# Half of an attention kernel's value matmuls moved into four column groups of TensorE

## The chip, the cores and the metric

The kernel runs on one core of a Trainium2 chip. The time is the device time of one execution in microseconds (us), the median of several runs. TensorE multiplies matrices into PSUM, ScalarE (ACT) applies functions, VectorE (DVE) does element work, GpSimd (POOL) does slower element work, SyncE (SP) starts transfers.

## The reference

Two rounds of a transformer block over x of 2048 rows and 512 columns: attention with 32 heads of 16 columns, then a feed-forward network (FFN) of 1792, each behind a layer norm and added to x. Both rounds use the same weights.

```python
def _A_ref(x, wqkv, wo):
    qkv = (x @ wqkv).reshape(B, S, 3, H, Dh).transpose(2, 0, 3, 1, 4)
    scores = einsum("bhqd,bhkd->bhqk", q, k) * Dh ** -0.5
    o = einsum("bhqk,bhkd->bhqd", softmax(scores), v)
    return o.transpose(0, 2, 1, 3).reshape(B, S, D) @ wo
...
x = x + _A_ref(_layernorm(x), A_wqkv, A_wo)
x = x + _B_ref(_layernorm(x), B_w1, B_w2)   # silu(x @ w1) @ w2
x = x + _A_ref(_layernorm(x), A_wqkv, A_wo)
x = x + _B_ref(_layernorm(x), B_w1, B_w2)
```

## The kernel before

Each layer runs in four **stages**, one for each chunk c of 512 query rows. A stage has eight **head blocks** (hb, four heads at a time), and each of these has sixteen **units** (kt), one for each tile of 128 keys. So a layer has 4 x 8 x 16 = 512 units, in the order of the list `units` (loop at line 576).

A unit does this. Four score matmuls (line 520) take K and Q of four heads, which lie 32 partitions apart, 17 rows each (16 columns of the head and one row that carries an offset, so that the exponentials stay in range), and write scores of 128 keys by 512 queries for each head, two heads to a PSUM tile `s_ps`. Two exponentials on ACT (line 585) read these tiles, 1024 elements in a partition, and write `p_sb`. Four value matmuls (line 532) multiply them with the values into `o_ps`, 128 partitions by 512, which is summed over all sixteen key tiles. Head j of the four owns partitions 32j to 32j+16 there: 16 value columns and the softmax's denominator, from a column of ones.

For that, the values stand in **padded blocks** `vd`: for each key tile and head 128 columns that are zero except for the head's 17. Each value matmul thus writes all 128 partitions and adds zeros to three heads. POOL copies the values from `v` (columns of 16) into the blocks (`vd_fill`, line 138), four key tiles at a time (`NG = 4`) in a ring of two (`NR = 2`); the zeros and ones are set once.

The order of instructions on TensorE, ACT and VectorE is the program's own order. In a unit's iteration of the loop, ACT gets the unit's two exponentials; TensorE gets the scores of the **next** unit, then the value matmuls of the second half of the last unit and of the first half of this one (`pend`), then **filler** work. There are three PSUM buffers of scores (`spool`), so the scores run at most a unit and a half ahead, and five buffers for `p_sb`.

The filler is a queue of small steps (`Pump`): K of the next head block (two matmuls a step, line 225, in the first stage of a layer only), Q of the next head block (lines 298 to 327), and from the second stage on the output projection of the last chunk (lines 362 to 383), its layer norm (lines 149 to 195), its FFN (lines 392 to 405, with a tanh on ACT, line 429) and in layer 0 the next layer's norm and values (line 269). `todo` spreads the steps over the stage's units. The K and Q steps stand in front, so that in the first stage of a layer the last units of a head block have no filler.

At a head's **boundary** (kt = 0) the value matmuls of the last head block are finished; VectorE casts `o_ps` to `oT` (line 573); and the next step in the queue, four transposes on TensorE (line 336), waits for this cast. At kt = 0 no value matmul of the new head is issued; all four follow at kt = 1, with two of that unit.

Outside the stages, a layer begins with K, Q and V for the first units and ends with the last chunk's projection and FFN.

Of the kernel before, what the change touches and what calls it, by code (L numbers as in the profile page):

```python
# [18 lines left out]
def kernel(  # L19
# [10 lines left out]
    nc = tc.nc  # L30
# [15 lines left out]
    EPS = 1e-5  # L46
    VS = DH + 1
    NG = 4
    NR = 2

    cpool = ctx.enter_context(tc.tile_pool(name="cpool", bufs=1))
    wpool = ctx.enter_context(tc.tile_pool(name="wpool", bufs=1))
    xpool = ctx.enter_context(tc.tile_pool(name="xpool", bufs=1))
    xnpool = ctx.enter_context(tc.tile_pool(name="xnpool", bufs=2))
    xtpool = ctx.enter_context(tc.tile_pool(name="xtpool", bufs=4))
    vpool = ctx.enter_context(tc.tile_pool(name="vpool", bufs=2))
# [6 lines left out]
    tpool = ctx.enter_context(tc.tile_pool(name="tpool", bufs=1))  # L63
    small = ctx.enter_context(tc.tile_pool(name="small", bufs=4))
    spool = ctx.enter_context(tc.tile_pool(name="spool", bufs=3, space=bass.MemoryType.PSUM))
    oppool = ctx.enter_context(tc.tile_pool(name="oppool", bufs=1, space=bass.MemoryType.PSUM))
# [2 lines left out]
    def wide(name):  # L69
        return spool.tile([P, 2, 512], FP32, name=name, tag="s")  # L70

    def narrow(name):
        return gpool.tile([P, 512], FP32, name=name, tag="g")
# [16 lines left out]
        nc.gpsimd.memset(E[32 * j : 32 * j + 16, 32 * j + 16 : 32 * j + 17], -1.0)  # L90
    eps_t = cpool.tile([P, 1], FP32, name="eps_t")
    nc.vector.memset(eps_t[:], EPS)
    onescol = cpool.tile([P, 1], FP32, name="onescol")
    mc_ps = narrow("mc_ps")
    nc.tensor.matmul(mc_ps[:, 0:1], lhsT=cw[0:1, 0:128], rhs=cw[0:1, 128:129], start=True, stop=True)
    nc.vector.tensor_copy(out=onescol[:], in_=mc_ps[:, 0:1])


    x_sb = xpool.tile([P, TT, D], BF16, name="x_sb")
# [12 lines left out]
    for ct in range(CT):  # L112
        nc.gpsimd.tensor_copy(
            out=wk_pad[:, ct, :, 0:DH],
# [3 lines left out]
            out=wq_pad[:, ct, :, 0:DH],  # L118
# [9 lines left out]
    vs = [vpool.tile([P, TT, D], BF16, name=f"v{i}", tag="v") for i in range(2)]  # L128
    vdq = []
    for i in range(NR):  # L130
        vd = xpool.tile([P, NG, 4, P], BF16, name=f"vd{i}")
        nc.gpsimd.memset(vd[:], 0.0)
        for j in range(4):
            nc.gpsimd.memset(vd[:, :, j, 32 * j + DH : 32 * j + DH + 1], 1.0)
        vdq.append(vd)


    def vd_fill(va, hb, g, slot):
        for j in range(4):
            h = 4 * hb + j  # L140
            nc.gpsimd.tensor_copy(  # L141
                out=vdq[slot][:, :, j, 32 * j : 32 * j + DH],
                in_=va[:, NG * g : NG * (g + 1), DH * h : DH * (h + 1)],
            )


# [119 lines left out]
    def v_mm(xnT, tt, ps, cts):  # L266
        tq = tt % 4
        for ct in cts:
# [2 lines left out]
                start=(ct == 0), stop=(ct == CT - 1),  # L271
            )

    def v_piece(cellx, tt, va):
        cell = {}

        def a():
            cell["ps"] = narrow("v_ps")
            v_mm(cellx["xnT"], tt, cell["ps"][:, :], (0, 1))

        def b():
            v_mm(cellx["xnT"], tt, cell["ps"][:, :], (2, 3))
            nc.vector.tensor_copy(out=va[:, tt, :], in_=cell["ps"][:, :])

        return [a, b]

    def v_two(xnT, tt, va):
        ps = wide("v2_ps")
        for i in range(2):
            v_mm(xnT, tt + i, ps[:, i, :], range(CT))  # L290
        nc.vector.tensor_copy(out=va[:, tt : tt + 2, :], in_=ps[:, :, :])

    def q_piece(xnTs, c, hb, QTs):
        cell = {}

# [221 lines left out]
    def emit_s(QT, hb, kt):  # L517
        tiles = [wide("s_ps") for _ in range(2)]
        for j in range(4):
            nc.tensor.matmul(  # L520
                tiles[j // 2][:, j % 2, :],
                lhsT=KT[32 * j : 32 * j + VS, hb, kt * P : (kt + 1) * P],
                rhs=QT[32 * j : 32 * j + VS, :],
                start=True,
                stop=True,
            )
        return tiles

    def emit_pv(o_ps, p_sb, kt, pr):
        for jj in range(2):  # L530
            j = 2 * pr + jj
            nc.tensor.matmul(  # L532
                o_ps[:, :],
                lhsT=vdq[kt // NG % NR][:, kt % NG, j, :],
                rhs=p_sb[:, jj, :],
                start=(kt == 0 and j == 0),
                stop=(kt == TT - 1 and j == 3),
            )
# [11 lines left out]
    for L in range(2):  # L550
# [14 lines left out]
        attn = None  # L565
        o_ps = None
        pend = []
        s_now = emit_s(QTs[0][0], 0, 0)
        left = 0

        def finish_heads(o_ps, hb, attn):
            oT = opool.tile([P, 512], BF16, name="oT", tag="oT")
            nc.vector.tensor_copy(out=oT[:], in_=o_ps[:])  # L573
            pump.front([heads_piece(oT, hb, attn)], state["begun"])

        for u, (c, hb, kt) in enumerate(units):
            if kt == 0:
                if hb == 0:
                    old_attn, attn_c = (attn, c - 1)
                    new_attn = apool.tile([P, 4, D], BF16, name="attn", tag="attn")  # L580

            ps = []
            for pr in range(2):
                p_sb = ppool.tile([P, 2, 512], BF16, name="p_sb", tag="p")
                nc.scalar.activation(  # L585
                    p_sb[:].rearrange("p a b -> p (a b)"),
                    s_now[pr][:].rearrange("p a b -> p (a b)"),
                    ACT.Exp,
                    scale=float(SCALE),
                )  # L590
                ps.append(p_sb)

            if u + 1 < len(units):
                nc_, nhb, nkt = units[u + 1]
                s_now = emit_s(QTs[nc_][nhb], nhb, nkt)

            if kt == 0:
                for args in pend:
                    emit_pv(*args)
                pend = []  # L600
# [10 lines left out]
                pend = [(o_ps, ps[0], 0, 0), (o_ps, ps[1], 0, 1)]  # L611
# [9 lines left out]
                pump.q[at:at] = [list(p) for p in must]  # L621
                left = at + len(must)
            else:
                pend.append((o_ps, ps[0], kt, 0))
                for args in pend:
                    emit_pv(*args)
                pend = [(o_ps, ps[1], kt, 1)]

            if kt % NG == 0 and u > 0 and u + NG * (NR - 1) < len(units):
                _, fhb, fkt = units[u + NG * (NR - 1)]  # L630
                vd_fill(va, fhb, fkt // NG, fkt // NG % NR)

            remaining = TT * HB - (hb * TT + kt)
            total = pump.steps()
# [1 line left out]
            todo = -(-(total + later) // remaining) if total else 0  # L636
            if left and kt < TT - 2 and pump.q:
                todo = max(todo, 1)
            pump_some(todo)
# [5 lines left out]
        for args in pend:  # L645
            emit_pv(*args)
        finish_heads(o_ps, HB - 1, attn)
        run(pump.q)
        pump.q = []
# [34 lines left out]
```

## Time and profile before

| | |
|---|---|
| runs | 2186.79 us median of 3 (2185.69 to 2189.19) |
| profiled execution, span | 2190.4 us |
| TensorE matmul busy | 1952.9 us (89%), 10355 records |
| ACT busy | 1943.4 us (89%) |
| VectorE busy | 558.6 us (26%) |
| POOL busy | 248.2 us (11%) |
| exponentials (line 585) | 2048, 1920.4 us busy |
| value matmuls (line 532) | 3909 records, 1045.1 us busy, mean 386 ns |
| score matmuls (line 520) | 4096, 575.3 us busy, mean 385 ns |
| mean granted clock of TensorE | 0.968 |
| DMA | 5 GB/s over the span |

The span runs from the first to the last instruction of one profiled execution. Busy time merges overlapping instructions: the 4096 score matmuls of 385 ns add up to far more than 575 us, because four of them run side by side. An instruction's duration is its latency, so a row of matmuls that follow each other closely takes less time than the sum of the means. 4096 value matmuls are issued; some records are missing from the trace. The granted clock is the share of its full rate at which TensorE was let run. The chain of waits follows the end of the span back to what released each step.

### The profile page before, as it was taken

What the parts mean: (1) busy time and instruction counts of PE and PEld (TensorE: products, weight loads), DVE (VectorE), ACT (ScalarE), POOL (GpSimd) and SP (SyncE); (2) the same over time, 40 slices, a digit from 0 to 9 for tenths busy, and PEclk for the clock granted to TensorE, in tenths of its full rate; (3) what the DMA queues carried; (4) which work ended last, traced back from release to release, by engine and by line L of the source; (5) the groups of instructions that cost most, each with busy time, mean ns of one, the idle gap of its engine ahead of it and who ended that gap; (6) DMA issues with size and microseconds to landing.
All of it is one profiled execution on the core that took longest, in us unless ns stands there. A gap on an engine that the chain in (4) does not pass through costs nothing.

```text
span 2190.4 us, 28490 instructions
## 1 busy us (share of the span) xinstructions
PE 1952.9 (89%) x10355; PEld 717.0 (33%) x10561; DVE 558.6 (26%) x1106; ACT 1943.4 (89%) x2152; POOL 248.2 (11%) x1055
## 2 busy tenths in 40 slices
PE   3999988999889998899778999998999989998996
PEld 1333323333333333333222333333333333333332
DVE  6323212112311133112343323131113111131114
ACT  0899989999799997999517999999999999999981
POOL 3111101111011110111000111111111111111100
PEclk9999999999899998999878999999999999999997
DMA  4000000000000000000000000000000000000000
GB/s 144 1 1 1 1 1 1 1 1 1 1 1 1 1 1 1 1 1 1 1 0 1 1 1 1 1 1 1 3 8 1 1 1 8 4 1 1 6 5 10
DMA packets 8477, 11.79 MB, mean 5 GB/s; under 512 B 400, under 2 KB 7312, under 8 KB 8336
## 3 DMA queue, kind: packets, MB, share of 16 engines
q1 hardware_dynamic: 7280, 8.39, 1.1%
q8 instruction: 82, 1.34, 0.3%
q10 hardware_dynamic: 1056, 1.57, 0.2%
q14 instruction: 59, 0.48, 0.1%
HBM read 7.86 MB, written 2.10 MB: 5 GB/s over the span
## 4 chain that ended last, share of the span: by engine, by line
PE 64%; ACT 21%; issue 8%; DVE 6%; DMA 0%; ACTq 0%; DVEq 0%
PE o_ps L532 30%; ACT p_sb L585 19%; PE s_ps L520 17%; PE y_ps L399 3%; PE k_ps L225 3%; PE q_ps L298 3%; PE h_ps L392 2%; PE y_ps L371 2%; PE v_ps L269 2%; ACT t_sb L429 1%; DVE st L149 1%; PE t_ps L194 1%; DVE oT L573 1%; PE at_ps L336 1%; DVE hT L477 1%
## 5 line engine op out<-in xcount | busy, mean ns | idle before, releaser
L585 ACT ACTIVATE p_sb<-s_ps 128x1024 bf16<-128x1024 f32 x2048 | 1920.4, 1237 | 123.3 <-PE s_ps L520 123.3
L532 PE MATMUL o_ps<-p_sb,vd 128*128 128x512 bf16 x3909 | 1045.1, 386 | 19.7 <-issue 15.5
L520 PE MATMUL s_ps<-QT,KT 17*128 17x512 bf16 x4096 | 575.3, 385 | 89.6 <-ACT p_sb L585 85.3
L532 PEld LDWEIGHTS <-vd 128*128 128x128 bf16 x4096 | 318.8, 98 | 484.8 <-issue 246.8
L141 POOL COPY vd<-v 128x64 bf16<-128x64 bf16 x1024 | 231.5, 239 | 1868.1 <-PE o_ps L532 1723.6
L520 PEld LDWEIGHTS <-KT 17*128 17x128 bf16 x4096 | 175.1, 91 | 591.1 <-issue 571.2
L573 DVE CAST oT<-o_ps 128x512 bf16<-128x512 f32 x64 | 44.3, 692 | 380.3 <-PE o_ps L532 380.3
L430 DVE SCALAR_TENSOR_TENSOR hT<-t_sb,h_ps 128x512 bf16<-128x512 f32 x84 | 57.5, 684 | 301.5 <-ACT t_sb L429 301.5
L399 PE MATMUL y_ps<-w_sb,hT 128*128 128x512 bf16 x445 | 128.0, 388 | 5.4 <-DVE hT L477 4.5
L392 PE MATMUL h_ps<-xnT,w_sb 128*128 128x512 bf16 x438 | 126.6, 387 | 3.2 <-DVE hT L477 1.4
L313 DVE CAST qc<-q_ps 128x512 bf16<-128x512 f32 x64 | 44.2, 691 | 173.0 <-PE q_ps L298 173.0
L242 DVE TENSOR_SCALAR KT<-k_ps,onescol 128x512 bf16<-128x512 f32 x56 | 42.0, 750 | 172.1 <-PE k_ps L225 172.1
L194 PE MATMUL t_ps<-ident,xn 128*128 128x128 bf16 x256 | 32.2, 271 | 57.1 <-DVE xn L182 55.4
L405 DVE SCALAR_TENSOR_TENSOR x_sb<-y_ps,x_sb 128x512 bf16<-128x512 f32 x32 | 22.1, 690 | 232.7 <-PE y_ps L399 232.7
L476 ACT ACTIVATE t_sb<-h_ps 128x1024 f32<-128x1024 f32 x14 | 14.3, 1024 | 75.1 <-PE h_ps L392 59.0
L298 PE MATMUL q_ps<-xnT,wq_pad 128*128 128x512 bf16 x255 | 77.0, 385 | 2.5 <-DVE attn L343 2.4
L225 PE MATMUL k_ps<-xnT,wk_pad 128*128 128x512 bf16 x254 | 78.7, 402 | 0.3 <-issue 0.2
L429 ACT ACTIVATE t_sb<-h_ps 128x512 f32<-128x512 f32 x84 | 76.9, 916 | 0.0
L399 PEld LDWEIGHTS <-hT 128*128 128x128 bf16 x448 | 44.3, 100 | 61.4 <-issue 6.1
L392 PEld LDWEIGHTS <-w_sb 128*128 128x128 bf16 x448 | 44.7, 100 | 58.4 <-issue 8.3
L327 DVE CAST QT<-q_ps 128x512 bf16<-128x512 f32 x64 | 44.2, 691 | 37.0 <-PE q_ps L322 37.0
L371 PE MATMUL y_ps<-wo_sb,aT 128*128 128x512 bf16 x126 | 40.8, 425 | 7.5 <-DVE aT L366 7.3
(58 smaller groups left out, 572.8 us busy)
## 6 DMA issues: line engine op xcount, KB each, us to landing
w_sb<-in_B_w_dram SPq DMA_DIRECT2D x2, 1792.0 KB, 15.0
x_sb<-in_A_x_dram SPq DMA_DIRECT2D x4, 512.0 KB, 9.8
out_dram<-x_sb SPq DMA_DIRECT2D x16, 128.0 KB, 1.7
wraw<-in_A_wqkv_dram ACTq DMA_DIRECT2D x1, 1024.0 KB, 7.6
wv_sb<-in_A_wqkv_dram ACTq DMA_DIRECT2D x1, 512.0 KB, 10.0
wo_sb<-in_A_wo_dram SPq DMA_DIRECT2D x1, 512.0 KB, 12.3
```

The costliest lines, as they stand in the source:

```text
L141: nc.gpsimd.tensor_copy(out=vdq[slot][:, :, j, 32 * j : 32 * j + DH], in_=va[:, NG * g : NG * (g + 1), DH * h : DH * (h + 1)],)
L225: nc.tensor.matmul(ps, lhsT=wk_pad[:, ct, 4 * hb : 4 * hb + 4, :].rearrange("p h s -> p (h s)"), rhs=xnT[:, ct, :], start=(ct == 0), stop= ...
L298: nc.tensor.matmul(cell["ps"][:, :], lhsT=wq_pad[:, ct, 4 * hb : 4 * hb + 4, :].rearrange("p h s -> p (h s)"), rhs=xnTs[c][:, ct, :], star ...
L371: nc.tensor.matmul(cell["ps"][:, :], lhsT=cell["aT"][:, ct, :], rhs=wo_sb[:, ct, :], start=(ct == 0), stop=(ct == CT - 1),)
L392: nc.tensor.matmul(ps, lhsT=w1_sb[:, ct, ft * P : (ft + 1) * P], rhs=xfT[:, ct, :], start=(ct == 0), stop=(ct == CT - 1),)
L399: nc.tensor.matmul(ps, lhsT=hT[:, ft, tq * P : (tq + 1) * P], rhs=w2_sb[:, ft, :], start=(ft == 0), stop=(ft == FT - 1),)
L429: nc.scalar.activation(t_sb[:, 0, :], hc["ps"][:, :], ACT.Tanh, scale=0.5)
L430: nc.vector.scalar_tensor_tensor(out=cell["hT"][:, ft, :], in0=t_sb[:, 0, :], scalar=1.0, in1=hc["ps"][:, :], op0=ALU.add, op1=ALU.mult,)
L520: nc.tensor.matmul(tiles[j // 2][:, j % 2, :], lhsT=KT[32 * j : 32 * j + VS, hb, kt * P : (kt + 1) * P], rhs=QT[32 * j : 32 * j + VS, :], ...
L532: nc.tensor.matmul(o_ps[:, :], lhsT=vdq[kt // NG % NR][:, kt % NG, j, :], rhs=p_sb[:, jj, :], start=(kt == 0 and j == 0), stop=(kt == TT - ...
L573: nc.vector.tensor_copy(out=oT[:], in_=o_ps[:])
L585: nc.scalar.activation(p_sb[:].rearrange("p a b -> p (a b)"), s_now[pr][:].rearrange("p a b -> p (a b)"), ACT.Exp, scale=float(SCALE),)
```

## The change

The key tiles 1, 3, 5, ... 15 of each head block (`COL`) no longer use padded blocks. Their values are read from `va`, the values in columns of 17 (16 and a one, set once by POOL), 32 columns at a time, and each of the four matmuls writes only its own 32 partitions of `o_ps`. (The 15 columns behind a head's 17 belong to the next head; what they add to `o_ps` lies in partitions that nobody reads.) The even tiles (`DIAG`) keep the padded blocks, which now hold two tiles (`NG = 2`). Both halves of an odd unit's value matmuls go into the iteration after it, before the first half of the even unit's. Score matmuls read 32 rows for 17; the added rows are zero. V goes into `va` with one cast for each tile of 128 rows, two where one was. Q's last step adds a constant column, and the exponential takes the same amount off again by a bias column. A path for exponentials on VectorE (`OFF`, `exp_passes`) is written but its list is empty: it issues nothing, and `late` and `passes` stay empty.

```diff
-    NG = 4
+    NG = 2
     NR = 2
+    COL = [1, 3, 5, 7, 9, 11, 13, 15]
+    DIAG = [kt for kt in range(TT) if kt not in COL]
+    KR = 32
+    OFF = []
...
+    nshift = cpool.tile([P, 1], FP32, name="nshift")
+    nc.vector.memset(nshift[:], -SHIFT)
+    nc.vector.tensor_scalar_mul(out=ccol[:], in0=onescol[:], scalar1=SHIFT / SCALE)
...
+    VW = VS * H + 32 - VS
+    for i in range(2):
+        va = xpool.tile([P, TT, VW], BF16, name=f"va{i}")
+        nc.gpsimd.memset(va[:], 1.0)
...
     def vd_fill(va, hb, g, slot):
+        k0, step = DIAG[NG * g], DIAG[1] - DIAG[0]
-                out=vdq[slot][:, :, j, 32 * j : 32 * j + DH],
-                in_=va[:, NG * g : NG * (g + 1), DH * h : DH * (h + 1)],
+                out=vdq[slot][:, :, j, 32 * j : 32 * j + VS],
+                in_=va[:, k0 : k0 + step * (NG - 1) + 1 : step, VS * h : VS * h + VS],
...
-        nc.vector.tensor_copy(out=va[:, tt : tt + 2, :], in_=ps[:, :, :])
+        for i in range(2):
+            nc.vector.tensor_copy(
+                out=v_dst(va, tt + i), in_=ps[:, i, :].rearrange("p (h d) -> p h d", d=DH)
+            )
...
-            nc.vector.tensor_copy(out=QTs[c][hb][:], in_=cell["ps"][:, :])
+            nc.vector.tensor_scalar(
+                out=QTs[c][hb][:], in0=cell["ps"][:, :], scalar1=ccol[:, 0:1], scalar2=None,
+                op0=ALU.add,
+            )
...
-                lhsT=KT[32 * j : 32 * j + VS, hb, kt * P : (kt + 1) * P],
-                rhs=QT[32 * j : 32 * j + VS, :],
+                lhsT=KT[32 * j : 32 * j + KR, hb, kt * P : (kt + 1) * P],
+                rhs=QT[32 * j : 32 * j + KR, :],
...
+    def emit_pv(o_ps, ps, hb, kt, prs, va):
+                if kt in COL:
+                    h = 4 * hb + j
+                    nc.tensor.matmul(
+                        o_ps[32 * j : 32 * j + 32, :],
+                        lhsT=va[:, kt, VS * h : VS * h + 32],
+                        rhs=ps[pr][:, jj, :],
+                        start=False,
+                        stop=(kt == TT - 1),
+                        skip_group_check=True,
+                    )
...
+                        bias=nshift[:],
                         scale=float(SCALE),
...
             else:
-                pend.append((o_ps, ps[0], kt, 0))
-                for args in pend:
-                    emit_pv(*args)
-                pend = [(o_ps, ps[1], kt, 1)]
+                flush(u)
+                elif kt in COL:
+                    pend.append((o_ps, ps, hb, kt, (0, 1)))
+                else:
+                    emit_pv(o_ps, ps, hb, kt, (0,), va)
+                    pend.append((o_ps, ps, hb, kt, (1,)))
```

More of the change, by code (lines that the diff above doesn't have):

```diff
@@ L55 @@
     xtpool = ctx.enter_context(tc.tile_pool(name="xtpool", bufs=4))
-    vpool = ctx.enter_context(tc.tile_pool(name="vpool", bufs=2))
     qpool = ctx.enter_context(tc.tile_pool(name="qpool", bufs=3))
@@ L63 @@
     tpool = ctx.enter_context(tc.tile_pool(name="tpool", bufs=1))
+    epool = ctx.enter_context(tc.tile_pool(name="epool", bufs=1))
     small = ctx.enter_context(tc.tile_pool(name="small", bufs=4))
@@ L92 @@
     nc.vector.memset(eps_t[:], EPS)
+    LOG2E = 1.4426950408889634
+    POLY = (-0.15703108, 12.31057503, 23.05391661, 37.67973007)
+    SHIFT = (127.0 - 6.207248627973487) / LOG2E
+    nshift = cpool.tile([P, 1], FP32, name="nshift")
+    nc.vector.memset(nshift[:], -SHIFT)
     onescol = cpool.tile([P, 1], FP32, name="onescol")
+    ccol = cpool.tile([P, 1], FP32, name="ccol")
     mc_ps = narrow("mc_ps")
@@ L127 @@
     amax = xpool.tile([P, HB], FP32, name="amax")
-    vs = [vpool.tile([P, TT, D], BF16, name=f"v{i}", tag="v") for i in range(2)]
+    VW = VS * H + 32 - VS
+    vs = []
+    for i in range(2):
+        va = xpool.tile([P, TT, VW], BF16, name=f"va{i}")
+        nc.gpsimd.memset(va[:], 1.0)
+        vs.append(va)
     vdq = []
@@ L132 @@
         nc.gpsimd.memset(vd[:], 0.0)
-        for j in range(4):
-            nc.gpsimd.memset(vd[:, :, j, 32 * j + DH : 32 * j + DH + 1], 1.0)
         vdq.append(vd)
     def vd_fill(va, hb, g, slot):
+        k0, step = DIAG[NG * g], DIAG[1] - DIAG[0]
         for j in range(4):
@@ L272, in v_mm, with v_dst @@
             )
+    def v_dst(va, tt):
+        return va[:, tt, 0 : VS * H].rearrange("p (h s) -> p h s", s=VS)[:, :, 0:DH]
     def v_piece(cellx, tt, va):
@@ L282, in b @@
             v_mm(cellx["xnT"], tt, cell["ps"][:, :], (2, 3))
-            nc.vector.tensor_copy(out=va[:, tt, :], in_=cell["ps"][:, :])
+            nc.vector.tensor_copy(
+                out=v_dst(va, tt), in_=cell["ps"][:, :].rearrange("p (h d) -> p h d", d=DH)
+            )
         return [a, b]
@@ L290, in v_two @@
             v_mm(xnT, tt + i, ps[:, i, :], range(CT))
-        nc.vector.tensor_copy(out=va[:, tt : tt + 2, :], in_=ps[:, :, :])
+        for i in range(2):
+            nc.vector.tensor_copy(
+                out=v_dst(va, tt + i), in_=ps[:, i, :].rearrange("p (h d) -> p h d", d=DH)
+            )
     def q_piece(xnTs, c, hb, QTs):
@@ L515, in pump_some, with emit_s @@
             state["begun"] = pump.step()
-    def emit_s(QT, hb, kt):
-        tiles = [wide("s_ps") for _ in range(2)]
-        for j in range(4):
+    def emit_s(QT, hb, kt, pr):
+        s_ps = wide("s_ps")
+        for jj in range(2):
+            j = 2 * pr + jj
             nc.tensor.matmul(
-                tiles[j // 2][:, j % 2, :],
-                lhsT=KT[32 * j : 32 * j + VS, hb, kt * P : (kt + 1) * P],
-                rhs=QT[32 * j : 32 * j + VS, :],
+                s_ps[:, jj, :],
+                lhsT=KT[32 * j : 32 * j + KR, hb, kt * P : (kt + 1) * P],
+                rhs=QT[32 * j : 32 * j + KR, :],
                 start=True,
@@ L526, in emit_s @@
             )
[L527 to L537, printed above, removed]
-            )
+        return s_ps
+    def emit_pv(o_ps, ps, hb, kt, prs, va):
+        for pr in prs:
+            for jj in range(2):
+                j = 2 * pr + jj
+                if kt in COL:
[7 more added lines that the diff above has]
+                        skip_group_check=True,
+                    )
+                else:
+                    d = DIAG.index(kt)
+                    nc.tensor.matmul(
+                        o_ps[:, :],
+                        lhsT=vdq[d // NG % NR][:, d % NG, j, :],
+                        rhs=ps[pr][:, jj, :],
+                        start=(kt == 0 and j == 0),
+                        stop=False,
+                        skip_group_check=True,
+                    )
@@ new lines, in exp_passes, with horner, split, broken @@
+    def exp_passes(s_ps, p_sb):
+        z = epool.tile([P, 1024], I32, name="z", tag="z")
+        m = epool.tile([P, 1024], FP32, name="m", tag="m")
+        y = epool.tile([P, 1024], FP32, name="y", tag="y")
+        flat = "p a b -> p (a b)"
+        def horner(out, in0, k, in1):
+            nc.vector.scalar_tensor_tensor(
+                out=out, in0=in0, scalar=POLY[k], in1=in1, op0=ALU.add, op1=ALU.mult
+            )
+        def split():
+            nc.vector.tensor_scalar(
+                out=z[:], in0=s_ps[:].rearrange(flat), scalar1=float(SCALE * LOG2E * 2**23),
+                scalar2=0.0, op0=ALU.mult, op1=ALU.max,
+            )
+        def broken():
+            nc.vector.tensor_scalar(
+                out=m[:].bitcast(I32), in0=z[:], scalar1=0x7FFFFF, scalar2=0x3F800000,
+                op0=ALU.bitwise_and, op1=ALU.bitwise_or,
+            )
+        def whole():
+            nc.vector.tensor_scalar(
+                out=z[:], in0=z[:], scalar1=0x7F800000, scalar2=None, op0=ALU.bitwise_and
+            )
+        return [
+            split, broken, whole,
+            lambda: horner(y[:], m[:], 0, m[:]),
+            lambda: horner(y[:], y[:], 1, m[:]),
+            lambda: horner(y[:], y[:], 2, m[:]),
+            lambda: horner(p_sb[:].rearrange(flat), y[:], 3, z[:].bitcast(FP32)),
+        ]
@@ L567 @@
         pend = []
-        s_now = emit_s(QTs[0][0], 0, 0)
+        late = []
+        passes = []
+        s_now = [emit_s(QTs[0][0], 0, 0, pr) for pr in range(2)]
         left = 0
@@ L574, in finish_heads, with flush @@
             pump.front([heads_piece(oT, hb, attn)], state["begun"])
+        def flush(u):
+            for args in pend:
+                emit_pv(*args, va)
+            pend.clear()
+            while late and late[0][0] <= u:
+                emit_pv(*late.pop(0)[1], va)
         for u, (c, hb, kt) in enumerate(units):
@@ L578 @@
                 if hb == 0:
-                    old_attn, attn_c = (attn, c - 1)
                     new_attn = apool.tile([P, 4, D], BF16, name="attn", tag="attn")
+            off = kt in OFF
             ps = []
             for pr in range(2):
[L584 to L590, printed above, removed]
+                if pr == 1 and off:
+                    p_sb = epool.tile([P, 2, 512], BF16, name="pd_sb", tag="pd")
+                    new = exp_passes(s_now[1], p_sb)
+                    new.pop(0)()
+                    passes += new
+                else:
+                    p_sb = ppool.tile([P, 2, 512], BF16, name="p_sb", tag="p")
+                    nc.scalar.activation(
+                        p_sb[:].rearrange("p a b -> p (a b)"),
+                        s_now[pr][:].rearrange("p a b -> p (a b)"),
+                        ACT.Exp,
+                        bias=nshift[:],
+                        scale=float(SCALE),
+                    )
                 ps.append(p_sb)
+            nxt_s = []
             if u + 1 < len(units):
                 nc_, nhb, nkt = units[u + 1]
-                s_now = emit_s(QTs[nc_][nhb], nhb, nkt)
+                nxt_s = [lambda pr=pr: emit_s(QTs[nc_][nhb], nhb, nkt, pr) for pr in range(2)]
+            s_now = [f() for f in (nxt_s[:1] if off else nxt_s)]
             if kt == 0:
-                for args in pend:
-                    emit_pv(*args)
-                pend = []
+                flush(u)
+                assert not late
                 if o_ps is not None:
@@ L610 @@
                 o_ps = oppool.tile([P, 512], FP32, name="o_ps", tag="o")
-                pend = [(o_ps, ps[0], 0, 0), (o_ps, ps[1], 0, 1)]
+                pend.append((o_ps, ps, hb, kt, (0, 1)))
                 must = []
@@ L623 @@
             else:
-                pend.append((o_ps, ps[0], kt, 0))
-                for args in pend:
-                    emit_pv(*args)
-                pend = [(o_ps, ps[1], kt, 1)]
-            if kt % NG == 0 and u > 0 and u + NG * (NR - 1) < len(units):
-                _, fhb, fkt = units[u + NG * (NR - 1)]
-                vd_fill(va, fhb, fkt // NG, fkt // NG % NR)
+                flush(u)
+                if off:
+                    s_now += [f() for f in nxt_s[1:]]
+                    emit_pv(o_ps, ps, hb, kt, (0,), va)
+                    late.append((u + 7, (o_ps, ps, hb, kt, (1,))))
+                elif kt in COL:
+                    pend.append((o_ps, ps, hb, kt, (0, 1)))
+                else:
+                    emit_pv(o_ps, ps, hb, kt, (0,), va)
+                    pend.append((o_ps, ps, hb, kt, (1,)))
+            if passes and not off:
+                passes.pop(0)()
+            elif passes and len(passes) > 6:
+                passes.pop(0)()
+            nd = len(DIAG)
+            if kt in DIAG and DIAG.index(kt) % NG == 0 and u > 0:
+                at_d = (c * HB + hb) * nd + DIAG.index(kt) + NG * (NR - 1)
+                if at_d < NQC * HB * nd:
+                    fhb, fd = at_d // nd % HB, at_d % nd
+                    vd_fill(va, fhb, fd // NG, fd // NG % NR)
             remaining = TT * HB - (hb * TT + kt)
@@ L638 @@
                 todo = max(todo, 1)
+            if off:
+                todo = 0
             pump_some(todo)
@@ L644 @@
                     pump_some(1)
-        for args in pend:
-            emit_pv(*args)
+        flush(len(units) + TT)
         finish_heads(o_ps, HB - 1, attn)
```

## The prediction

> **What bounds the kernel now.** I read the rows of ScalarE's exponential line first, cut at the eight stages (four query chunks of 512 rows in each of two layers). Columns: window, its length, ACT busy (instructions), granted TensorE clock, DMA share, GB/s.
>
> ```profile
> 65.28:303.19 237.91, 235.16 (x257) 0.99 0.00 1
> 303.19:559.20 256.01, 241.99 (x258) 0.97 0.00 1
> ...
> 1161.34:1401.43 240.09, 235.20 (x257) 0.98 0.00 1
> 1401.43:1644.91 243.48, 240.93 (x258) 0.99 0.01 3
> ```
>
> ACT is busy almost throughout, and busy time alone does not say whether it is the limit. So I took the chain of waits in a stretch without filler work, where each unit shows one exponential and the next one starts when it should:
>
> ```profile
> 1220.16 1.29 ACT p_sb L585
> ...
> 1221.97 1.31 ACT p_sb L585
> ```
>
> Two exponentials take 1.81 us, 0.905 each. Where a tanh of the FFN stands between two, it adds 0.47 (ACT's timeline: tanh starts at 692.30, the exponential behind it at 692.77). The floor of a stage is therefore 256 x 0.905 = 231.7 us, with 14 tanhs 238.3. Excess over it: 6.2 in the first stage, 17.7 in each of the next three (53.3 in all), 8.4, 5.2, 3.9 and 4.3 in layer 1: **81 us**. Whatever TensorE is spared, no more can be won, and the 216 us outside the stages (65.3 of start, 89.9 between layers, 60.8 of end) hold no attention loop.
>
> Where the 81 us lie: the first 43.8 us of the stages at 303, 559 and 815 hold 32 exponentials (29.0), 14.8 lost each, 44.4 in all; the other 61 head blocks lose 36.9, 0.60 each. Inside a block TensorE with filler work runs at ACT's own pace, as the chain in layer 1 shows:
>
> ```profile
> 1206.78 0.43 PE s_ps L520 x4
> 1207.21 0.97 PE o_ps L532 x4
> 1208.18 0.43 PE k_ps L225 x2
> ```
>
> That is 1.83 us against 1.81. The 0.60 is lost at the head's boundary, where TensorE, in order, waits for VectorE's cast and then has six value matmuls before the next scores:
>
> ```profile
> 1225.55 0.55 PE o_ps L532 x2
> ...
> 1226.12 0.70 DVE oT L573
> ...
> 1226.87 0.40 PE at_ps L336 x4
> 1227.27 0.33 PE s_ps L520 x4
> 1227.60 1.40 PE o_ps L532 x6
> 1229.00 0.43 PE k_ps L225 x2
> ```
>
> **The clock** is the second thing to read. Columns: window, length, PE, PEld, DVE, ACT, POOL busy (instructions), granted clock.
>
> ```profile
> 1192.90:1196.30 3.40, 2.46 (x18) 0.69 (x17) 0.95 (x2) 3.40 (x5) 0.91 (x4) 1.00 0.00 0
> 1196.30:1199.70 3.40, 3.40 (x12) 0.98 (x8) 0.42 (x1) 2.11 (x3) 0.00 (x0) 0.50 0.03 5
> ...
> 1223.70:1227.11 3.41, 2.47 (x15) 0.78 (x14) 0.69 (x1) 3.41 (x5) 0.91 (x4) 1.00 0.00 0
> 1227.11:1230.53 3.42, 3.42 (x23) 1.31 (x21) 0.68 (x2) 3.26 (x4) 0.00 (x0) 1.00 0.00 0
> ```
>
> Two head boundaries, alike to a few hundredths; after one the clock is 0.50 for a window of 3.4 us, after the other it is not. The second holds some eight passes of 512 columns (six padded value matmuls, four scores side by side, the start of the transposes), 8 x 0.216 = 1.73 us, half of the window. So boundaries now sit at the edge of a threshold near one half.
>
> **The change part by part.** A padded value matmul takes 0.216 in a row (0.43 for two, filler rows). Two units, an odd and an even key tile, now take 3.66. After it:
> - The iteration of an odd tile: scores 0.43, two padded matmuls of the tile before 0.43, filler 0.43 = 1.29.
> - The iteration of an even tile: scores 0.43, the block of four narrow matmuls C, two padded 0.43, filler 0.43, and one more change of array mode. The scores' four matmuls are one pass of 0.22 (a lone pass: "q_ps L322 0.22") and take 0.43, so entering and leaving cost 0.21; one change is half, 0.10.
> - C is not in the trace: at least a pass, 0.22; at most four in a row, 0.97. I take 0.43, the scores' block, the nearest row, since it too is four narrow matmuls side by side. Then the even iteration is 1.82 and the pair 3.11, 0.55 less, far under ACT's 3.62.
>
> Inside a block this earns nearly nothing: ACT is late next, at 0.905. At a boundary the two matmuls become C (-0.12) and the six become four (-0.43); I count 0.43 of the 0.60. At full clock: 61 x 0.43 = **-26**. In the long openings (303, 559, 815) 16 units are eight pairs; five at full clock save 0.44 (the odd 0.97 becomes 0.53), two at half clock 0.86, one lies under the LN chain on VectorE (329.75 to 336.5): 3.9 each, **-12**.
>
> Against this stands the clock. In the boundary window above, six padded matmuls become two plus C: eight passes become five, 32% of the window. I found none this thin inside the stages that kept the clock. In the filler-free tail of a head of stage 0 a pair of units is seven passes in 3.62 us, 42%, also below the edge. What a half-clock window costs is measured: head blocks that have one last 31.2 us, the others 29.6: 1.6. Of the six padded matmuls that stood in it (2.66 against 1.40) four remain, which saves 0.85. A boundary at half clock then loses 0.60 + 1.6 - 0.85 = 1.35, 0.75 **more** than now; at full clock 0.43 less. Boundaries break even when 36% fall. I take all 14 of stage 0 (no filler in the tail) and a third of the 47 others, 30 of 61: 30 x 0.75 - 31 x 0.43 = **+9**. Four boundaries are cold today and save 0.85: **-3**.
>
> [...]
>
> Small parts. Weight loads: 98 ns each, under matmuls now; if those of the block lay open, 4 x 0.098 = 0.39 makes the pair 3.50, still below 3.62: 0. [...] Scores over 32 rows: matmuls of 17 and of 128 rows last 385 and 386 ns: 0. V's first cast, two of 512 for one of 1024: 2 x 0.691 - 1.225 = 0.157, x8: **+1**, at most, as TensorE sets that stretch. QT's add: 0.750 (the KT row) for 0.691, on an engine busy 26%: 0. The exponential's bias is another column of the same size; the page's fill of a 128x1 constant 0.0 is the one of before: 0. POOL: two fills of 8944 elements, by 3.52 per 4096, 7.7 each; POOL ends at 17.5 today and then at about 32, V's first cast is at 49: hidden by 17. POOL's copies stay 1024, now 34 elements for 64: 0. DMAs stay. A new wait: both tiles of an odd unit are read one iteration later, and the second exponential two units on needs the buffer (five in the ring). It starts 0.905 after the first, C ends 0.43 after the scores: free at full clock, about even at half. Behind it on ACT stand all exponentials, and TensorE's scores for them.
>
> Sum: -12 + 9 - 3 + 1 = -5. The profiled execution spans 2190.4, the median of the runs is 2186.8, 3.6 below: 2190.4 - 5 - 3.6 = **2182 us**. This kernel's measurement tells 0.2% (4.4 us) from no change.
>
> **The rivals.**
> - The clock holds (the narrow block counts as much as a padded one). For it: boundaries such as that at 1223.7 hold now. Against: five passes for eight. -26 - 12 - 8 (the four cold ones save 2.0 each) + 1 = -45: 2142.
> - Slower, one mechanism: TensorE, lighter, falls to half clock at every boundary and stays there for two windows in half of them, since waiting for VectorE's cast leaves the first half-clock window unfilled as well (the stage openings show pairs of such windows: 0.84 of clock over 43.8 us). In the second window a unit with filler takes about 2.6 us (1.56 doubled, less the waits that don't grow) for 1.81, 1.3 units: +1.0. 61 x 0.75 + 30 x 1.0 = 76, less 14: 2190.4 + 62 - 3.6 = 2249. It decides from about 15 us more than the 36% give, that is when 60% of the boundaries fall.
> - The narrow matmuls run one after another (C = 0.97): the change doesn't do what it says. The pair is 1.29 + 2.36 + 0.10 = 3.75, above ACT's 3.62, in 104 pairs with filler of the two stages 0 and 84 of the FFN's second product: 188 x 0.13 = +24, clock as now: 2212. For: no row shows column groups. Against: row groups do overlap (575 us for 4096 matmuls of 385 ns).
>
> **How the numbers follow.** Forecast (2168 to 2197) 0.42: faster 0.20, same 0.13, slower 0.09. Clock holds 0.22, faster. Two windows 0.20, slower. In a row 0.12, slower. The ring or the bias costs after all 0.04, slower. Together: faster 0.42, same 0.13, slower 0.45. The range 2145 to 2235 leaves out half of the first rival and half of the second.
>
> **What would show it.** The narrow block in the chain near 0.43 (0.22 to 0.97); exponentials at 1.81 per unit in all blocks; the span's mean clock below 0.968, with 0.50 windows behind most boundaries of stage 0 and a third of the others; head blocks of 29.2 where it holds and 30.3 where it falls; openings of about 40 instead of 43.8. It is wrong if the exponential's own pace moves, or if the clock falls in the middle of blocks that have filler.

## The result and the profile after

The changed kernel takes **2382.3 us** (median of 4 runs, 2376.85 to 2387.54) against 2187.99 for the kernel before on the same chip (4 runs): a ratio of **1.0889 [1.0866, 1.0913]**. The forecast was 2182, the range 2145 to 2235. The profiled execution spans 2375.1 us at a mean granted clock of 0.920, that is 184.7 more than the 2190.4 of before.

ScalarE's exponential in the list of the costliest groups of the kernel before (busy us, mean ns of one, idle time before them and what ended it), then the exponential and the narrow value matmuls in that of the changed kernel:

```profile
L585 ACT ACTIVATE p_sb<-s_ps 128x1024 bf16<-128x1024 f32 x2048 | 1920.4, 1237 | 123.3 <-PE s_ps L520 123.3
```

```profile
L684 ACT ACTIVATE p_sb<-s_ps,nshift 128x1024 bf16<-128x1024 f32 x2048 | 2092.1, 1393 | 116.6 <-PE s_ps L554 116.2
...
L569 PE MATMUL o_ps<-p_sb,va 128*32 128x512 bf16 x2048 | 217.8, 416 | 0.0
```

The same number of exponentials, 2048, keeps ACT busy for 2092.1 us where it was 1920.4. The inputs say why they differ: `s_ps,nshift`, where the row of before has `s_ps` alone. The stages 0 and 1 of both layers, by the exponential's rows (window, length, ACT busy, clock, DMA, GB/s):

```profile
72.81:337.74 264.93, 258.41 (x257) 0.89 0.00 1
337.74:609.79 272.05, 263.93 (x258) 0.97 0.00 1
...
1250.44:1516.80 266.36, 258.46 (x257) 0.88 0.00 1
1516.80:1782.01 265.21, 261.68 (x258) 0.95 0.01 3
```

Every one of the eight stages is longer by 16 to 27 us, ACT is busy for nearly all of each, and the clock is lower, most in the first stage of a layer. The chain of waits in a unit without filler gives the new pace:

```profile
1311.19 1.27 ACT p_sb L684
...
1313.18 1.29 ACT p_sb L684
```

That is 1.99 us for two exponentials, where it was 1.81. From the starts of all exponentials, the median spacing is 0.997 us after and 0.904 before. With these the 184.7 come apart (spans; "excess" is the spacing of the exponentials above the median and above 0.47 per tanh, summed over the stages; the tanhs' own time in the stages is the same in both and left out):

| | before | after | difference |
|---|---|---|---|
| 2048 exponentials at ACT's pace | 0.904 each | 0.997 each | +190.5 |
| start of the first exponential | 65.23 | 72.76 | +7.5 |
| excess in the stages | 82.7 | 71.3 | -11.4 |
| between the layers, and the end | 151.5 | 149.7 | -1.8 |

The sum is 184.8 with the rounding. ACT's pace alone is more than the whole difference; what the rest of the change was meant to do must be looked for in the small rows.

### The profile page after: what moved, and what is told of

Its sections match the earlier page's. It is cut to its first block, busy times and chain, and to the rows that moved or that the text cites. A ratio compares the mean times of both kernels' runs of the same rounds, so it can differ in the third digit from the quotient of the medians.

```text
span 2375.1 us, 28507 instructions
## 1 busy us (share of the span) xinstructions
PE 1936.7 (82%) x10364; PEld 601.2 (25%) x10561; DVE 574.3 (24%) x1116; ACT 2125.6 (89%) x2152; POOL 251.4 (11%) x1049
## 4 chain that ended last, share of the span: by engine, by line
PE 42%; ACT 38%; issue 13%; DVE 6%; DMA 0%; ACTq 0%; DVEq 0%
ACT p_sb L684 36%; PE s_ps L554 15%; PE o_ps L579 11%; PE o_ps L569 5%; PE k_ps L247 2%; PE h_ps L425 2%; ACT t_sb L462 1%; PE y_ps L404 1%; PE q_ps L328 1%; PE y_ps L432 1%; PE v_ps L291 1%; DVE st L171 1%; DVE oT L659 1%; DVE xn L204 1%; PE at_ps L369 1%
## 5 line engine op out<-in xcount | busy, mean ns | idle before, releaser
L684 ACT ACTIVATE p_sb<-s_ps,nshift 128x1024 bf16<-128x1024 f32 x2048 | 2092.1, 1393 | 116.6 <-PE s_ps L554 116.2
L554 PE MATMUL s_ps<-QT,KT 32*128 32x512 bf16 x4096 | 769.2, 403 | 279.8 <-ACT p_sb L684 262.6
L579 PE MATMUL o_ps<-p_sb,vd 128*128 128x512 bf16 x1907 | 628.7, 412 | 22.2 <-issue 21.9
L163 POOL COPY vd<-va 128x34 bf16<-128x34 bf16 x1024 | 221.4, 219 | 2046.6 <-PE o_ps L579 1689.6
L554 PEld LDWEIGHTS <-KT 32*128 32x128 bf16 x4096 | 192.7, 91 | 967.3 <-issue 949.5
L569 PE MATMUL o_ps<-p_sb,va 128*32 128x512 bf16 x2048 | 217.8, 416 | 0.0
L579 PEld LDWEIGHTS <-vd 128*128 128x128 bf16 x2048 | 126.2, 100 | 262.2 <-issue 252.6
L432 PE MATMUL y_ps<-w_sb,hT 128*128 128x512 bf16 x425 | 120.9, 380 | 5.3 <-DVE hT L510 4.5
L569 PEld LDWEIGHTS <-va 128*32 128x32 bf16 x2048 | 53.3, 94 | 128.9 <-issue 128.9
L509 ACT ACTIVATE t_sb<-h_ps 128x1024 f32<-128x1024 f32 x14 | 14.3, 1024 | 77.1 <-PE h_ps L425 63.7
L462 ACT ACTIVATE t_sb<-h_ps 128x512 f32<-128x512 f32 x84 | 71.3, 848 | 0.0
L357 DVE TENSOR_SCALAR QT<-q_ps,ccol 128x512 bf16<-128x512 f32 x64 | 48.1, 751 | 57.5 <-PE q_ps L352 57.5
```

The lines of the kernel that those rows point to most:

```text
L163: nc.gpsimd.tensor_copy(out=vdq[slot][:, :, j, 32 * j : 32 * j + VS], in_=va[:, k0 : k0 + step * (NG - 1) + 1 : step, VS * h : VS * h + VS],)
L432: nc.tensor.matmul(ps, lhsT=hT[:, ft, tq * P : (tq + 1) * P], rhs=w2_sb[:, ft, :], start=(ft == 0), stop=(ft == FT - 1),)
L462: nc.scalar.activation(t_sb[:, 0, :], hc["ps"][:, :], ACT.Tanh, scale=0.5)
L554: nc.tensor.matmul(s_ps[:, jj, :], lhsT=KT[32 * j : 32 * j + KR, hb, kt * P : (kt + 1) * P], rhs=QT[32 * j : 32 * j + KR, :], start=True, ...
L569: nc.tensor.matmul(o_ps[32 * j : 32 * j + 32, :], lhsT=va[:, kt, VS * h : VS * h + 32], rhs=ps[pr][:, jj, :], start=False, stop=(kt == TT ...
L579: nc.tensor.matmul(o_ps[:, :], lhsT=vdq[d // NG % NR][:, d % NG, j, :], rhs=ps[pr][:, jj, :], start=(kt == 0 and j == 0), stop=False, skip ...
```

## The experiments

Three theories stood after the result. **Bias:** the exponential is slower because its bias is now a column in SBUF; its rivals are the constant in Q, which changes the numbers that are exponentiated, and contention for buffers. **Clock:** TensorE, lighter, falls to half clock at the boundaries and the scores come late, which the slower exponential now hides in part. **Fill:** POOL's long fills of `va` hold VectorE up at the start. Ratios are against the kernel before on the same chip; "half clock" counts the stretches of the trace in which the granted clock was 0.50, and their total.

| run | median us | ratio to before | spacing | first exponential | excess | half clock |
|---|---|---|---|---|---|---|
| before | 2186 to 2189 | | 0.904 | 65.23 | 82.7 | 17, 143 us |
| after | 2382.3 | 1.0889 [1.0866, 1.0913] | 0.997 | 72.76 | 71.3 | 53, 382 |
| e1_no_bias | 2211.0 | 1.0104 [1.0078, 1.0131] | 0.904 | 73.49 | 94.4 | 45, 276 |
| e3_imm_bias | 2210.8 | 1.0108 [1.0081, 1.0134] | 0.904 | 73.73 | 96.9 | 47, 293 |
| e2_before_bias | 2356.6 | 1.0766 [1.0733, 1.0799] | 0.996 | 63.59 | 59.8 | 20, 150 |
| e4_no_bias_17 | 2248.0 | 1.0277 [1.0251, 1.0304] | 0.904 | 73.41 | 130.6 | 65, 498 |
| e5_small_fill | 2208.7 | 1.0094 [1.0081, 1.0108] | 0.904 | 69.66 | 94.4 | 45, 276 |
| e11_fill_on_dve | 2203.5 | 1.0085 [1.0068, 1.0101] | 0.904 | 63.62 | 94.2 | 45, 280 |
| e6_warm_cast | 2187.1 | 0.9995 [0.9986, 1.0004] | 0.904 | 68.69 | 77.7 | 29, 153 |
| e7_warm_tail | 2186.7 | 1.0001 [0.9991, 1.0010] | 0.904 | 67.86 | 73.9 | 27, 167 |
| e8_all_padded | 2178.6 | 0.9966 [0.9954, 0.9979] | 0.903 | 69.26 | 69.2 | 10, 95 |
| e9_before_32 | 2173.7 | **0.9937 [0.9925, 0.9950]** | 0.904 | 65.16 | 68.4 | 11, 105 |
| e10_before_32_warm | 2192.6 | 1.0037 [1.0025, 1.0050] | 0.904 | 64.40 | 89.0 | 9, 82 |

Several forecasts of these runs were missed. e1 and e3 ended 1 us above their range, e4 lost 37 us where 20 was the most expected, e9 gained 14 where 2 to 10 were expected, e5 gained 2 of the 8 forecast, e11 ended a little under its range, and e10 was slower than both of its theories allowed.

### The bias column: e1, e3, e2

e1 takes the column and Q's constant out of the changed kernel. e3 keeps Q's constant and gives the bias as a number in the instruction. e2 adds both the column and Q's constant to the kernel before.

```diff
 e1, against the changed kernel
-            nc.vector.tensor_scalar(
-                out=QTs[c][hb][:], in0=cell["ps"][:, :], scalar1=ccol[:, 0:1], scalar2=None,
-                op0=ALU.add,
-            )
+            nc.vector.tensor_copy(out=QTs[c][hb][:], in_=cell["ps"][:, :])
...
-                        bias=nshift[:],
 e3, against the changed kernel
-                        bias=nshift[:],
+                        bias=float(-SHIFT),
 e2, against the kernel before: nshift, ccol and Q's add as in the change, and
+                    bias=nshift[:],
```

> The changed kernel without the pair of shifts: Q's last step is the plain cast again and the exponential has no bias column; everything else stays. Theory 1 (the bias column makes each exponential 0.093 us longer, 2048 of them, 190 us): exponentials again 0.904 apart, time 2382 - 190 = 2192, between 2170 and 2210. Rival A (narrow value matmuls and the lower clock hold ScalarE up): exponentials stay at 0.997 and the time at 2370 to 2385. Rival B (reading 32 rows or the narrow blocks' reads disturb ScalarE's reads of PSUM): the same as A.

> The changed kernel with the same shift as a constant in the instruction instead of a column in SBUF; Q's added constant stays, so the numbers that are computed are the same. Theory 1, if it is the reading of a column that costs: as without the bias, 2192 (2170 to 2210), exponentials 0.904 apart. If it is the bias itself, or the other values that reach the exponential: 2382 and 0.997. Rivals A and B: 2370 to 2385.

> The kernel before with only the pair of shifts added: a bias column for the exponential, a constant column added to Q. Theory 1: exponentials 0.997 apart, 32 of them 31.9 us in place of 28.9; the 37 us that head blocks lose now shrink since TensorE is no longer as slow as ScalarE: 2188 + 190 - 20, between 2345 and 2380. Rivals A and B: 2188, within 5.

Measured: without the column 2211.0, with the same bias as a number 2210.8, with the column in the old kernel 2356.6. The exponential's row in e1, e3 and e2, in this order:

```profile
L681 ACT ACTIVATE p_sb<-s_ps 128x1024 bf16<-128x1024 f32 x2048 | 1920.2, 1307 | 131.7 <-PE s_ps L551 129.8
```

```profile
L684 ACT ACTIVATE p_sb<-s_ps 128x1024 bf16<-128x1024 f32 x2048 | 1920.3, 1303 | 134.3 <-PE s_ps L554 132.8
```

```profile
L593 ACT ACTIVATE p_sb<-s_ps,nshift 128x1024 bf16<-128x1024 f32 x2048 | 2098.5, 1442 | 110.1 <-PE s_ps L528 109.9
```

Wherever `nshift` stands among the inputs, ACT is busy for 2092 to 2098 us, and 1920 where it does not, in either kernel. e3 has the same numbers to exponentiate as the changed kernel and Q's add, so neither the values nor the add is the cause; e2 has neither column groups nor 32 rows of scores, so contention from these is not. The bias theory is shown: 0.093 us for each of 2048 exponentials, 190 us. Of these 23 are given back, in the change (excess 94.4 without the column, 71.3 with it) as in the old kernel (82.7 and 59.8), about half in the openings of the stages 1 to 3 of layer 0 and half in the other head blocks. That TensorE has more slack at a slower pace is the likely reason; no run takes it apart. In the spans 165 us remain, in the change as in e2.

### The start: e5 and e11

e5 is e1 with the fill cut to what has to be one (the ones columns and the 15 trailing columns); e11 lets VectorE write the same.

```diff
 e5, against e1
-        nc.gpsimd.memset(va[:], 1.0)
+        nc.gpsimd.memset(
+            va[:, :, 0 : VS * H].rearrange("p t (h s) -> p t h s", s=VS)[:, :, :, DH : DH + 1], 1.0
+        )
+        nc.gpsimd.memset(va[:, :, VS * H : VW], 1.0)
 e11, against e5: nc.vector.memset in both places
```

> The changed kernel without the two shifts, and POOL fills only the columns of ones and the 15 columns behind the last head instead of the whole value tiles (2 x 8944 elements). Theory 2 (VectorE's normalising instruction xn stands still while POOL's long fill runs, 7.86 us for one of 0.4): the first exponential comes 8 us earlier, near 65 instead of 73.5, and the time falls by 8, to 2203. Rival (the start is late for another reason, such as the added instructions on VectorE): no change, 2211 within 3.

> The small-fill kernel with the columns of ones written by VectorE, before x has landed, instead of by POOL. Theory 2 (VectorE's xn stands still while POOL fills SBUF): the xn of 7.0 us shrinks to 2 us or less, the first exponential comes at 65 to 66 instead of 69.7, 2204 to 2206 in place of 2208.7. Rival (the late start is not POOL's): 69 to 70, and 2208 or more.

The fourth normalisation of the first rows on VectorE's timeline (start, duration), and the fill beside it on POOL's, in the kernel before, in the changed kernel, in e5 and in e11:

```profile
13.43 2.10 DVE L182 TENSOR_SCALAR xn<-x_sb,mvb,rstd 128x512 bf16<-128x512 bf16 x1
13.58 3.69 POOL L132 MEMSET vd<- 128x2048 bf16 x2
```

```profile
13.44 7.85 DVE L204 TENSOR_SCALAR xn<-x_sb,mvb,rstd 128x512 bf16<-128x512 bf16 x1
13.60 15.18 POOL L150 MEMSET va<- 128x8944 bf16 x2
```

```profile
13.26 7.00 DVE L207 TENSOR_SCALAR xn<-x_sb,mvb,rstd 128x512 bf16<-128x512 bf16 x1
13.42 2.27 POOL L150 MEMSET va<- 128x512 bf16 x1
15.29 0.60 POOL L153 MEMSET va<- 128x240 bf16 x1
```

```profile
13.30 1.25 DVE L207 TENSOR_SCALAR xn<-x_sb,mvb,rstd 128x512 bf16<-128x512 bf16 x1
```

The same instruction takes 0.40 us when POOL is at rest (in the kernel before at 21.88 us), and here it lasts as long as POOL's fill beside it. One fill of `va` is half of 15.18: 13.60 + 7.59 = 21.19, and VectorE's instruction ends at 13.44 + 7.85 = 21.29. The kernel before shows the same at a smaller size: 13.58 + 1.85 = 15.43, and 13.43 + 2.10 = 15.53. The transposes of these rows, and with them the start, wait for it. e5's cure was half a miss: its fills write scattered elements, 2.27 us for 512, and they follow each other without a pause, so VectorE stood through all four and the two of `vd` behind them (to 20.10) and the first exponential came at 69.66 (e1: 73.49), not at 65. With only the short fills of `vd` beside it (e11: two from 13.46, 1.98 together, so the first ends near 14.45) it is 1.25 us, to 14.55, and the first exponential comes at 63.62. The fill theory is shown: the long fill costs 8 us at the start against the kernel before, and 10 against e11.

How POOL's fill holds VectorE up, no run here shows.

### The clock: e4, e8, e9

e4 is e1 with 17 rows of scores again. e8 is e5 with all key tiles padded, so it keeps the 32 rows, the new V columns and the new order. e9 is the kernel before with nothing but 32 rows.

```diff
 e4, against e1
-    KR = 32
+    KR = 17
 e8, against e5
-    COL = [1, 3, 5, 7, 9, 11, 13, 15]
+    COL = []
 e9, against the kernel before
-                lhsT=KT[32 * j : 32 * j + VS, hb, kt * P : (kt + 1) * P],
-                rhs=QT[32 * j : 32 * j + VS, :],
+                lhsT=KT[32 * j : 32 * j + KR, hb, kt * P : (kt + 1) * P],
+                rhs=QT[32 * j : 32 * j + KR, :],
```

> As the first of these, without bias column and without Q's constant, and scores read 17 rows again in place of 32. If rows of scores count for the granted clock: a lower mean clock than with 32 rows and some us more, up to 20. If 32-row groups count whole, or rows cost nothing: the same time within 4 us.

> The small-fill kernel with every key tile in padded blocks (two tiles to a block buffer, so POOL copies twice as often) and none in column groups; values in columns of 17, 32 rows of scores, no shifts. It gives the column groups' own price. Theory (the groups make TensorE lighter and the clock falls at boundaries, which costs more than the spared work): as the kernel before with 32 rows, 2174, and up to 5 more for the start, 2174 to 2182, so the groups cost about 30. Rival (something else of the change, such as the layout of V or the fills, holds the rest of the loss): 2200 to 2209, as with the groups.

> The kernel before with scores over 32 rows instead of 17 and nothing else. If rows count for the clock (17 rows made the changed kernel 37 us slower): fewer than the 17 windows at half clock, mean clock above 0.968, and 2 to 10 us less than before, mostly in the first stages of layers. If they matter only through something in the narrow blocks: 2188 within 3.

First the block itself, in a boundary of e1 that keeps the clock (chain of waits):

```profile
1206.09 0.39 PE o_ps L566 x4
...
1206.49 0.70 DVE oT L656
...
...
1207.64 0.33 PE s_ps L551 x4
1207.97 0.97 PE o_ps L576 x4
1208.94 0.43 PE k_ps L247 x2
```

Four narrow matmuls take 0.39 (0.33 elsewhere), and four padded ones stand where six stood: the boundary's path became shorter, as meant. A boundary of the changed kernel that loses the clock, as the last window of 3.4 us at full clock and the one that follows it (length, then PE, PEld, DVE, ACT, POOL busy, then the clock) and as chain:

```profile
1315.80:1319.21 3.41, 2.29 (x14) 0.58 (x11) 0.00 (x0) 3.41 (x5) 0.76 (x4) 1.00 0.00 0
1319.21:1322.62 3.41, 2.58 (x16) 1.05 (x13) 1.37 (x3) 3.41 (x5) 0.00 (x0) 0.50 0.00 0
```

```profile
1318.92 0.39 PE o_ps L569 x4
...
1321.23 1.82 PE o_ps L579 x4
1323.05 0.85 PE k_ps L247 x2
```

PE is busy for 2.29 us of 3.41, and then the clock is 0.50, here for two windows (to 1326.03): four padded matmuls take 1.82 for 0.97, K's two 0.85 for 0.43.

What the parts are worth: e5 against e8, the column groups alone: 2208.7 against 2178.6, **+30 us**, of which 25 are excess in the stages (94.4 against 69.2), with 45 stretches of half clock against 10. e4 against e1, rows alone: 17 for 32 cost **37 us** and bring 65 stretches for 45. e9 against before: 32 rows gain **14 us** (17 stretches to 11). The exponential's row in e5 and then in e8 shows what ACT waited for the scores, 130.0 and 105.3:

```profile
L684 ACT ACTIVATE p_sb<-s_ps 128x1024 bf16<-128x1024 f32 x2048 | 1920.2, 1307 | 131.8 <-PE s_ps L554 130.0
```

```profile
L684 ACT ACTIVATE p_sb<-s_ps 128x1024 bf16<-128x1024 f32 x2048 | 1921.2, 1249 | 105.3 <-PE s_ps L554 105.3
```

The windows of stage 0 of layer 0, e1 and then e4 (columns as above):

```profile
73.54:314.55 241.01, 212.57 (x1199) 63.55 (x1200) 62.88 (x89) 235.62 (x257) 27.29 (x126) 0.96 0.00 1
```

```profile
73.46:318.00 244.54, 219.98 (x1192) 63.36 (x1192) 62.87 (x89) 235.18 (x255) 26.79 (x124) 0.89 0.00 1
```

The matmuls are the same but for 15 rows of each score matmul that only multiply zeros; the clock is 0.96 with them and 0.89 without. So what decides is not the time that PE is busy alone: the rows in use count. Two windows of e4, each with the one behind it, also show that PE's busy time does not decide (their starts lie 275 x 3.413 us apart; in the traces of before and after, too, all stretches of half clock, 17 and 53, begin a whole multiple of 3.413 us apart):

```profile
463.33:466.74 3.41, 2.19 (x16) 0.90 (x14) 1.29 (x2) 3.41 (x5) 0.00 (x0) 1.00 0.02 5
466.74:470.16 3.42, 3.42 (x22) 1.10 (x20) 0.68 (x2) 3.42 (x5) 0.84 (x4) 1.00 0.00 0
...
1402.00:1405.41 3.41, 2.73 (x16) 0.67 (x15) 0.00 (x0) 3.41 (x5) 0.86 (x4) 1.00 0.02 5
1405.41:1408.83 3.42, 2.50 (x15) 0.80 (x15) 1.35 (x3) 2.89 (x5) 0.00 (x0) 0.50 0.00 0
```

Behind 2.19 us of busy PE the clock holds, and behind 2.73 it falls. e9 is the fastest kernel of this study, 0.63% under the kernel before.

### Can the clock be held? e6, e7, e10

e6 is e5 with three spare full-width matmuls, into a tile that nobody reads, issued while TensorE would wait for the cast; e7 adds three more steps of two such in the tails of stage 0's head blocks, where there is no filler; e10 puts e6's three into e9.

```diff
 e6 against e5, e10 against e9: in the step with the four transposes
         def a():
+            w_ps = narrow("w_ps")
+            for _ in range(3):
+                nc.tensor.matmul(
+                    w_ps[:, :], lhsT=ident[:, :], rhs=wo_sb[:, 0, :], start=True, stop=True
+                )
 e7 against e6 (warm issues two such matmuls)
+                if c == 0:
+                    must += [[warm] for _ in range(3)]
```

> As the small fill, and TensorE does three matmuls of 512 columns into a spare PSUM tile, whose result nobody reads, while it waits for VectorE's cast at a head's boundary (0.65 us of a wait of 0.75). Theory 3 (what is left of the slowdown is the half clock behind boundaries, since a window there is too thin): fewer windows at half clock than the 45 without it, head blocks at 29.0 instead of 30.5, 10 to 30 us less than the small fill alone: 2173 to 2193. Rival (the clock does not go by such matmuls, or a fallen clock costs nothing here): equal to the small fill or, by the added work, a few us more.

> As the one before, and in the first stage of each layer three more steps of two such matmuls in the last units of a head block, which have no filler. Theory 3: the tail of these blocks no longer lets the clock fall; head blocks of the first stages at 29.0, up to 10 us less than without these steps. Rival: the same time, since a fallen clock in the tail is over before work stands behind it.

> The kernel before with 32 rows of scores and the three extra matmuls during the cast at a head's boundary. If the 0.67 us that its boundaries lose were due to the clock, they would lose less and the time would fall by up to 10, to 2164; if they are due to the six value matmuls in a row, nothing changes there, the few windows at half clock that are left go or stay, and the time is 2170 to 2177.

e6 is 21.6 us faster than e5: 29 stretches of half clock for 45, and six of the eight head blocks of stage 0, layer 1 lose 0.41 each where most lost 1.6. In the spans it is 23.4, of which 16.7 are excess and 5.7 lie between the layers and at the end. A boundary of stage 0 in e6 (chain of waits):

```profile
130.34 0.70 DVE oT L664
...
131.48 0.33 PE s_ps L559 x4
131.81 0.97 PE o_ps L584 x4
```

These are full-clock durations (0.97 for four padded matmuls, not 1.82): the clock is what made most of those boundaries dear. In the later stages more of the blocks lose 0.72 where those that held lost 0.2 to 0.5: there, as it seems, TensorE had work during the cast, and the spare matmuls only add to it. Net, e6 equals the kernel before. e7 measured the same as e6 (2186.7 and 2187.1): with the cast filled, filling the tails too earns nothing. e10 is 19 us slower than e9, although it has less half clock (82 us for 105): many of its blocks in later stages lose 1.2 for 0.5. The 0.67 per boundary of stage 0 did not move, so with all blocks padded that loss does not belong to the clock. The chain of e9 puts it on the cast (0.70) and the six value matmuls (1.40), which no run took away on their own.

## Why the prediction was wrong, point by point

Two rows of the kernel before, on which the first point rests:

```profile
L154 ACT ACTIVATE std<-mvb,eps_t 128x4 f32<-128x4 f32 x4 | 1.2, 298 | 30.7 <-DVE mvb L150 30.7
L476 ACT ACTIVATE t_sb<-h_ps 128x1024 f32<-128x1024 f32 x14 | 14.3, 1024 | 75.1 <-PE h_ps L392 59.0
```

- **"The exponential's bias is another column of the same size": 0, measured +165 in the spans** (190 from the pace, 23 given back, 2 elsewhere). This is the step that failed. It took a fill of a 128x1 constant in the page as a sign that the old exponential already read a column. The exponential's own row (the first of the section on the result) spoke against that: `p_sb<-s_ps`, one input. And the profile of before had a row with such a column, the square root of the norm, with `eps_t` among its inputs, and a tanh without one (the two rows above this list). The square root of 4 elements takes 298 ns, the tanh of 1024 elements 1024 ns; at the exponentials' 0.904 us for 1024 elements that leaves at least 120 ns that do not depend on the size. By this estimate the column costs between 0 and 298 - 120 = 178 ns, times 2048: bounds of 0 and +365, with the measured 190 in the middle. The prediction did say that it is wrong "if the exponential's own pace moves", and gave "The ring or the bias costs after all" 0.04.
- **POOL's fills "hidden by 17": 0, measured +8 at the start.** It asked who waits for POOL's result and not who runs beside it. The 2.10 us of the fourth `xn` in the kernel before, three times its neighbours (0.64 to 0.74) and five times the 0.40 of one with POOL at rest, beside a fill of 3.69 for two, was the row to see.
- **"Scores over 32 rows: 0" as duration right** (a pass is still 0.33 to 0.43 in the chain), but the clock was not asked: -14 us in the old kernel, -37 in the changed one.
- **C = 0.43: 0.33 to 0.39.** Column groups do run side by side (four padded matmuls in a row take 0.97); the rival of narrow matmuls in a row fell. The 0.10 for a change of array mode was an estimate from two rows (0.43 and 0.22); no run takes it apart.
- **Boundaries and clock, +9 and -3: about +18** (excess outside the three openings, e1 against before). The direction was right and the count near: in e1 34 of the 61 blocks hold more than 1 us of half clock (30 were forecast), 13 of the 16 in the first stages of the layers and 21 of the other 45. These lose 1.42 on average (1.35 forecast), the other 27 lose 0.28 (0.17 forecast). That the count came out is in part luck: the forecast gave the rows of the scores no part in the clock, and with 17 rows (e4) 45 of the 61 fall and lose 1.83. The rival that the clock holds fell; the one of two windows too, as 31 of the 38 stretches of half clock inside e1's stages last one window (in the changed kernel 21 of 48 last longer). The threshold near one half of a window was an estimate from two windows of before; no run shows it, and e4 kept the clock behind 2.19 us of busy PE and lost it behind 2.73.
- **Openings -12: -6** (14.85 lost in each before, 12.9 in each in e1).
- **Nothing won inside the blocks, QT's add 0: right.** The median spacing is 0.904 in e1, ACT's own, and e3 with the add equals e1 without it. In e1 130 of the 132 us of ACT's idle time before exponentials are put down to the scores, so no wait for the ring of `p_sb` shows.

Without bias and without POOL's fill (e11) the change still costs 0.85% [0.68, 1.01]: the part that was forecast at -5 us is +10 in the span (2200.2 against 2190.4), and it is excess (82.7 to 94.2). So the sign of this part was wrong too. In medians, from before to after: 32 rows -14, new V layout and its smaller fill +5 (e9 to e8; 4 of them a later start), column groups +30 (e8 to e5), the long fill +2 (e5 to e1), the bias +171: 194, as measured. The change pays three prices (the bias column, the fill, the lower clock of the column groups) on a path that ACT bounds; the one part that helps is the padding of the score matmuls with zeros.

**Open:** what exactly the granted clock follows. Rows count (65 stretches of half clock in e4 for 45 in e1, 11 in e9 for 17 before). With column groups the clock falls more often (45 stretches in e5, 10 in e8), but they also shorten PE's busy time, so that columns and time are not told apart here.

## What to carry to other kernels

Before an edit of the instruction that sets the pace, read its inputs in its own row: a constant that moves from the instruction to a column in SBUF cost 93 ns each time here, 2048 times, and a number in the instruction did the same for nothing (e3). Where another engine is the limit, work taken off TensorE earned nothing inside the blocks and cost its clock; look at the windows around its waits, and try rows of zeros, which gained in both kernels, before spare matmuls, which gained in one (e6) and lost in the other (e10). For work on an idle engine ask not only who waits for its result but who runs beside it.

## What the runs showed of the hardware

- Rows of zeros raise the granted clock: 15 more rows in each score matmul took stage 0's clock from 0.89 (e4) to 0.96 (e1). They took no time of their own: 4096 score matmuls keep PE busy for 575.3 us, mean 385 ns, with 17 rows (before) and for 575.0, mean 384, with 32 (e9).
- A VectorE instruction of 0.40 us stood for 7.85 beside one POOL fill of 7.59 (after), and for 7.00 through six shorter fills that followed each other (e5).
- A slower pace of ACT gave back part of its own price: 23 of 190 us, in both kernels.
- Spare matmuls at the boundaries lowered the half clock (105 us to 82) and still lost 19 us (e10 against e9).
